# Loading queries and keys in token order for an attention stage ahead of two feed-forward layers

## The chip, the cores and the metric

The kernel runs on one core of a Trainium2 chip. The metric is the time of one execution on the device in microseconds (us); less is better. Below, TensorE is the engine for matrix products and transposes, VectorE, ScalarE and GpSimd do elementwise work, and SP is the queue from which most transfers are started. In rows of the profile they are called PE (weight loads: PEld), DVE, ACT, POOL and SP.

## The reference

For 4 batches, 8 heads, 576 tokens and head dimension 64, two attentions are added; then two feed-forward layers follow on 2304 tokens of width 512 with 2048 hidden features.

```python
q_d = q.reshape(B, H, Sd, factor, D).mean(axis=3)      # factor = 4; k_d, v_d in the same way
out_up = np.repeat(sm_attn(q_d, k_d, v_d), factor, axis=2)
mask = np.abs(pos[:, None] - pos[None, :]) < factor
scores = np.where(mask, scale * np.matmul(q, k.transpose(0, 1, 3, 2)), -1000000000.0)
out_local = np.matmul(softmax(scores), v)
x = out_up + out_local                                  # then, for each layer:
h = x @ w_in                                            # g = h * sigmoid(h) in layer 1, elu(h) in layer 2
return g @ w_out
```

The weights come as float64.

## The kernel before

The attention is done for 16 pairs of heads: pair i is two heads of one batch, whose 64 dimensions each lie on partitions 0 to 63 and 64 to 127. `attention(i)` is a generator; each `yield` ends one step, and `step()` takes one step of each live pair in turn. The first four pairs (batch 0) run side by side at the start, each begun three steps behind the one before, with matrix products of zeros between them (`warm`). Then the feed-forward layers begin, and the steps of pairs 4 to 15 are put between their matrix products by `tick`: one at a time in the first two blocks of tokens and three at a time after that. A pair has 19 steps.

The feed-forward products are done by `g1` (line 452) and `g2` (lines 503 and 505) on weights that are kept as two parts. The weights are turned from float64 to float32 by `decode_w` (lines 152 to 159 on VectorE, 143 on ScalarE) and split by `split_w` (169 and 171); the first 16 tiles of them are prepared during the first attention pairs and the first block.

The order of the instructions on every engine is the order in which the program gives them; nothing is reordered, so an instruction that waits holds back all behind it on its engine. Transfers on SP and on ScalarE's queue are started in that order too.

What the change touches in `attention`:

- `load_rows` loads queries (which = 0), keys (1) and values (2) of a pair: eight neighbouring tokens on each of 72 partitions. For the first four pairs a partition gets runs of 2 KB, and `set_beside` (line 220, VectorE) copies them so that the two heads' dimensions lie side by side. From pair 4 on the load itself sets them side by side, in runs of 256 bytes.
- 16 transposes of 72 tokens (line 281, tile `pst`, four to a PSUM bank), four copies out of PSUM with a stride (line 282, ScalarE), and two sums over four tokens (line 288, VectorE) give `qT`, `kT` and the pooled `qD`, `kD`.
- GpSimd adds the values (lines 296 and 297: `vt`, `vd`). After these the loads of the next pair are started.
- `psl` (line 308) holds the banded scores: 20 products whose operands lie alternately on the two halves of the partitions and whose results go alternately to two halves of PSUM's partitions.
- The pooled scores `psd` (line 334): for each head two products over 64 partitions and then a maximum on VectorE (341) that is scaled by a separate instruction (344) before ScalarE's exponential (347).
- The tiles `qT`, `kT`, `vt`, `E`, `ED`, `aT` and `aD` share seven buffers (`ring`); a tile waits until a buffer is free.
- `psu` (line 391) holds the weighted pooled values: four products of 72 partitions whose results go in turn to the two halves of PSUM's partitions.

Of the kernel before, what the change touches and what calls it, by code (L numbers as in the profile page):

```python
# [21 lines left out]
def attention_moe_moe2_kernel(ctx, tc, q, k, v, wi1, wo1, wi2, wo2, out):  # L22
# [10 lines left out]
    NBS = (2 * P, 3 * P)  # tokens of a block in each layer  # L33
# [5 lines left out]
    PSCALE = SCALE / (FAC * FAC)  # L39
    EPS = 1e-9  # L40
    MASKED = -1e9
    WIN = 64
    PACES = (1.0, 0.9, 0.7)  # steps of attention per tick in the first block, the second and the others
    DECODE_PACE = 1.5  # small steps of the first weights per tick
    N_EARLY = 9  # tiles of weights that may be prepared before the first product
    WARM, FILL = 9, (8, 4, 4, 4)
    GROUP = 3  # steps of attention at a time after the first two blocks
    LAG = 3  # tiles of hidden features between the two products
    # 2^16 times the float32 whose bits are the high word of the float64 that is float32's largest.
# [4 lines left out]
    # Windows of the banded attention: key start, query start, first useful query of each.  # L54
# [27 lines left out]
    def constants():  # L82
# [24 lines left out]
    # Tiles of weights in the order of their use; each is loaded, decoded and split in turn.  # L107
# [72 lines left out]
    # The first batch's four pairs go side by side and borrow memory that is not in use yet: tokens  # L180
    # of the later batches in x32, the parts of x, and the partial results.
    borrowed = {}

    def borrow(i, name):
        at, n = {"qT": (S, S), "kT": (2 * S, S), "qD": (3 * S, SD), "kD": (3 * S + SD, SD), "vd": (3 * S + 2 * SD, 2 * SD)}[name]
        return x32[:, pairs[i][1], at:at + n][:, :2 * 2 * D if name == "vd" else n]

    def load_rows(i, which, engine=None):
        b, h0 = pairs[i][0], 2 * pairs[i][1]
        src = (q, k, v)[which]  # L190
        if i in (1, 2) and which < 2:
            t = xs.tile([P, KC * NBM], F32R, tag=("xh", "xl")[which], name=f"rows{which}").bitcast(F32)
            borrowed[2 * i - 2 + which] = t
            t = t[:, :4 * FAC * D].rearrange("p (r e) -> p r e", e=2 * D)
        elif i == 3 and which == 0:
            borrowed["y"] = yp.tile([P, 4 * NBM], F32, tag="y", name="rows0")
            t = borrowed["y"][:, :4 * FAC * D].rearrange("p (r e) -> p r e", e=2 * D)
        else:
            t = nat.tile([P, 2 * FAC, 2 * D], F32, tag="nat", name=f"rows{which}", bufs=3)
        # Eight neighbouring tokens on a partition; the two heads' dimensions of q and k side by side.  # L200
        if which == 2 or i < NPAIR:
            t = t.rearrange("p r e -> p (r e)").rearrange("p (h e) -> p h e", h=2)
            (engine or nc.sync).dma_start(t[:HS], src[b, h0:h0 + 2].rearrange("h (p r) d -> p h (r d)", r=2 * FAC))
        else:
            (engine or nc.sync).dma_start(
                t[:HS].rearrange("p r (h d) -> p r h d", h=2),
                src[b, h0:h0 + 2].rearrange("h (p r) d -> p r h d", r=2 * FAC),
            )
        loaded[i, which] = t

    # The first batch's rows come whole, a head after the other, for its loads are waited for.
    beside = {}

    def set_beside(i, which):
        src = loaded[i, which].rearrange("p h (a r d) -> p a r h d", a=2, r=FAC)
        for a in range(2):
            tag = ("wh0", "wl0", "wh1", "wl1")[2 * which + a]
            t = wpool.tile([P, DM], F32R, tag=tag, name="beside").bitcast(F32).rearrange("p (r e) -> p r e", r=FAC)
            beside[i, which, a] = t
            nc.vector.tensor_copy(t[:HS].rearrange("p r (h d) -> p r h d", h=2), src[:HS, a])  # L220
# [39 lines left out]
    def ring(name, n):  # L260
        return att.tile([P, NW * WIN], F32, tag="ring", name=name, bufs=7)[:, :n]

    def attention(i):
        b, pr = pairs[i]
        # Transposes: dimensions of both heads on the partitions, tokens along the row.
        tT = []
        tD = []
        if i < NPAIR:
            set_beside(i, 0)
            set_beside(i, 1)  # L270
        for which, nm in enumerate("qk"):
            src = loaded.pop((i, which))
            t = borrow(i, f"{nm}T") if i < NPAIR else ring(f"{nm}T", S)
            for a in range(2):
                if i < NPAIR:
                    rows = beside[i, which, a]
                else:
                    rows = src[:, a * FAC:(a + 1) * FAC, :]
                ps = bank("pst")
                for r in range(FAC):  # L280
                    nc.tensor.transpose(ps[:, r * HS:(r + 1) * HS], rows[:HS, r, :], ident[:HS, :HS])  # L281
                nc.scalar.copy(
                    t.rearrange("p (m a r) -> p a r m", a=2, r=FAC)[:, a],
                    ps[:, :HALF].rearrange("p (r m) -> p r m", r=FAC),
                )
                yield
            d = borrow(i, f"{nm}D") if i < NPAIR else att.tile([P, SD], F32, tag=f"{nm}D", name=f"{nm}D")
            nc.vector.reduce_sum(d, t.rearrange("p (m r) -> p m r", r=FAC), axis=AX.X)
            tT.append(t)
            tD.append(d)  # L290
        # Values pooled over FAC neighbours (their sum).
        vt = ring("vt", 2 * 2 * 2 * D).rearrange("p (n r d) -> p n r d", n=4, r=2)
        vd = borrow(i, "vd") if i < NPAIR else att.tile([P, 4 * D], F32, tag="vd", name="vd", bufs=3)
        vd = vd.rearrange("p (n d) -> p n d", n=4)
        vn = loaded.pop((i, 2)).rearrange("p h (a r d) -> p (h a) r d", a=2, r=FAC)
        nc.gpsimd.tensor_tensor(vt[:HS], vn[:HS, :, 0:2, :], vn[:HS, :, 2:4, :], ALU.add)
# [5 lines left out]
        # Banded scores, two windows of queries stacked on the partitions.  # L302
# [11 lines left out]
        for j in range(2):  # L314
            nc.vector.scalar_tensor_tensor(
                E[:, :, j, :], psl[j][:, :NW // 2 * WIN].rearrange("p (s w) -> p s w", w=WIN), SCALE, mask,
# [9 lines left out]
        # Pooled scores.  # L326
# [4 lines left out]
        for j in range(2):  # L331
            ps = bank("psd")
            for a in range(2):
                nc.tensor.matmul(  # L334
                    ps[:HS, a * SD:(a + 1) * SD],
# [3 lines left out]
                )  # L339
            nm = att.tile([P, 2], F32, tag="nm", name="nm", bufs=4)  # L340
# [3 lines left out]
            nc.vector.tensor_scalar_mul(nm[:HS], nm[:HS], PSCALE)  # L344
            yield
            for a in range(2):
                nc.scalar.activation(
                    ED[:HS, j, a, :], ps[:HS, a * SD:(a + 1) * SD], AF.Exp, bias=nm[:HS, a:a + 1], scale=PSCALE,
# [9 lines left out]
        # The pooled values are sums of FAC: their factor goes into the weights.  # L358
# [8 lines left out]
        # Weights transposed: keys on the partitions.  # L367
# [18 lines left out]
        # Weighted values; dimensions of both heads on the partitions.  # L386
# [56 lines left out]
    def g1(u, tick):  # L443
# [17 lines left out]
        if layer == 0:  # L461
            # 2 silu(h) = (tanh(h / 2) + 1) h
# [3 lines left out]
        else:  # L466
            # elu(h) = max(exp(min(h, 0)) - 1, h)
# [11 lines left out]
    def g2(u, tick):  # L479
# [53 lines left out]
    with tc.manual_schedule():  # L533
# [10 lines left out]
        # Products of zeros keep TensorE at its full clock where it has nothing else to do yet.  # L544
# [8 lines left out]
        # Work that is spread between the matrix products, a small step at a time.  # L553
# [26 lines left out]
        # The first tiles of weights: decoded and split at once, two of them in turn.  # L580
# [34 lines left out]
        def step():  # L615
            # Some pairs in turn, each some stages behind the one before.
# [48 lines left out]
        def advance():  # L665
            # The rest of a tile's elementwise work, a step at a time.
# [93 lines left out]
```

## Time and profile before

| what | value |
|---|---|
| time, median of 3 runs | 1003.09 us (1002.03 to 1005.25) |
| span of the profiled execution, first to last instruction | 1000.2 us |
| TensorE busy | 970.6 us, 97% |
| VectorE busy | 583.9 us, 58% |
| ScalarE busy | 429.2 us, 43% |
| GpSimd busy | 368.8 us, 37% |
| mean granted TensorE clock | 0.970 |

The profile prints no time of the profiled execution but its span; the median of the runs is 2.9 us above that. Busy time is counted for each engine from its own instructions. Shares over the whole span mix stages with different limits, so a stage is read by its own stretch of time. A matmul's length in the timeline overlaps with the next one, so the price of a matmul is read from the distance between starts.

### The profile page before, as it was taken

To read this page: it belongs to the slowest core of one execution; us is meant where nothing else is said; L and a number is where in the kernel's file an instruction comes from. 1 tells how busy PE (TensorE), PEld (TensorE's weight loads), DVE (VectorE), ACT (ScalarE), POOL (GpSimd) and SP (SyncE) were. 2 spreads that over 40 slices of the span, in tenths; PEclk is the share of its full clock that TensorE was granted. 3 is DMA by queue.
4 is the path that set the end of the run, shared out by engine and by line. 5 is a ranking of instruction groups with operands and counts; after the bars stand their busy time and mean duration, and the time that the engine had idled before them with its cause. 6 is when DMAs were issued, how large, how long until landed. Compare 5 with 4: busy or idle time off the path is not lost.

```text
span 1000.2 us, 18822 instructions
## 1 busy us (share of the span) xinstructions
PE 970.6 (97%) x7517; PEld 893.8 (89%) x7517; DVE 583.9 (58%) x1076; ACT 429.2 (43%) x1032; POOL 368.8 (37%) x375
## 2 busy tenths in 40 slices
PE   7887799999999999999999999999999999999998
PEld 4567688999999999999999999999999999999997
DVE  7999864555548966876322267677643544434432
ACT  4555546456445556444333354333333533223321
POOL 3756654543522235222222362222223622222221
PEclk9677799999999999999999999999999999999999
DMA  8555644333205541343100001232000011101111
GB/s 210 129 131 134 155 96 107 84 75 88 62 8 154 182 130 56 117 125 117 53 23 22 22 22 43 78 112 64 32 32 32 1 64 64 44 20 64 64 38 57
DMA packets 81687, 77.76 MB, mean 78 GB/s; under 512 B 51520, under 2 KB 67904, under 8 KB 81600
## 3 DMA queue, kind: packets, MB, share of 16 engines
q1 hardware_dynamic: 81288, 75.97, 26.6%
q8 instruction: 59, 0.97, 0.4%
q10 hardware_dynamic: 312, 0.59, 0.2%
q14 instruction: 28, 0.23, 0.1%
HBM read 62.39 MB, written 14.16 MB: 77 GB/s over the span
## 4 chain that ended last, share of the span: by engine, by line
PE 89%; DVE 8%; DMA 1%; issue 1%; ACT 1%; POOL 0%; ACTq 0%; DVEq 0%; POOLq 0%
PE ph L452 40%; PE y L503 21%; PE y L505 20%; PE pso L403 2%; PE psd L334 1%; PE pst L281 1%; DVE wf L157 1%; DVE wf L152 1%; DVE wf L153 1%; DMA rows<-in_k_dram 1%; PE psl L308 1%; DVE wf L159 1%; PE psu L391 1%; DVE nm L344 1%; PE psE L374 1%
## 5 line engine op out<-in xcount | busy, mean ns | idle before, releaser
L475 POOL TENSOR_TENSOR gl<-t,gh 128x256 fp32r<-128x256 f32 (+1 forms) x240 | 215.9, 900 | 527.2 <-ACT gh L473 514.0
L452 PE MATMUL ph<-xh,wh 128*128 128x256 f32 (+1 forms) x960 | 279.4, 309 | 1.6 <-DVE t L465 1.6
L452 PE MATMUL ph<-xl,wh 128*128 128x256 f32 (+1 forms) x960 | 278.8, 308 | 0.0
L452 PEld LDWEIGHTS ph<-xh,wh 128*128 128x128 f32 x960 | 183.9, 192 | 7.9 <-DVE t L465 1.8
L452 PEld LDWEIGHTS ph<-xl,wh 128*128 128x128 f32 x960 | 184.0, 192 | 4.6 <-issue 0.4
L452 PE MATMUL ph<-xh,wl 128*128 128x256 f32 (+1 forms) x960 | 179.9, 307 | 0.3 <-POOL wl L171 0.3
L503 PE MATMUL y<-gh,wh 128*128 128x256 f32 x576 | 169.3, 294 | 0.0
L473 ACT CAST gh<-t 128x256 fp32r<-128x256 f32 (+1 forms) x240 | 107.9, 449 | 132.8 <-DVE t L465 83.8
L503 PE MATMUL y<-gl,wh 128*128 128x256 f32 x576 | 163.9, 285 | 0.0
L503 PE MATMUL y<-gh,wl 128*128 128x256 f32 x576 | 163.8, 284 | 0.0
L452 PEld LDWEIGHTS ph<-xh,wl 128*128 128x128 f32 x960 | 149.6, 192 | 1.3 <-POOL wl L171 0.6
L465 DVE SCALAR_TENSOR_TENSOR t<-t,ph 128x256 f32<-128x256 f32 x144 | 60.1, 418 | 141.8 <-ACT t L463 141.6
L469 ACT ACTIVATE t<-t 128x384 f32<-128x384 f32 x96 | 50.5, 526 | 211.1 <-DVE t L468 211.0
L468 DVE TENSOR_SCALAR t<-ph 128x384 f32<-128x384 f32 x96 | 53.4, 556 | 126.1 <-PE ph L452 126.0
L503 PEld LDWEIGHTS y<-gh,wh 128*128 128x128 f32 x576 | 111.4, 193 | 3.7 <-issue 3.1
L505 PE MATMUL y<-wl,gh 128*128 128x512 f32 x288 | 113.9, 396 | 0.0
L505 PE MATMUL y<-wh,gl 128*128 128x512 f32 x288 | 113.7, 395 | 0.0
L463 ACT ACTIVATE t<-ph 128x256 f32<-128x256 f32 x144 | 55.5, 385 | 133.1 <-PE ph L452 130.2
L505 PE MATMUL y<-wh,gh 128*128 128x512 f32 x288 | 111.9, 389 | 0.0
L503 PEld LDWEIGHTS y<-gl,wh 128*128 128x128 f32 x576 | 111.5, 194 | 0.0
L503 PEld LDWEIGHTS y<-gh,wl 128*128 128x128 f32 x576 | 111.4, 193 | 0.0
L471 DVE SCALAR_TENSOR_TENSOR t<-t,ph 128x384 f32<-128x384 f32 x96 | 53.2, 554 | 56.8 <-ACT t L469 56.8
(89 smaller groups left out, 1306.8 us busy)
## 6 DMA issues: line engine op xcount, KB each, us to landing
ws<-in_moe_w_in_dram SPq DMA_DIRECT2D x32, 512.0 KB
ws<-in_moe_w_out_dram SPq DMA_DIRECT2D x32, 512.0 KB
rows<-in_q_dram SPq DMA_DIRECT2D x16, 288.0 KB
rows<-in_v_dram SPq DMA_DIRECT2D x16, 288.0 KB
yp<-yo SPq DMA_DIRECT2D x9, 512.0 KB
part<-yp SPq DMA_DIRECT2D x9, 512.0 KB
yp<-yo SPq DMA_DIRECT2D x6, 768.0 KB
part<-yp SPq DMA_DIRECT2D x6, 768.0 KB
```

The costliest lines, as they stand in the source:

```text
L152: nc.vector.tensor_scalar(tf, tf, 2.0, W_MAX, op0=ALU.max, op1=ALU.min)
L403: nc.tensor.matmul(ps[j * D:(j + 1) * D, o:o + n], loaded[i, 3][j * WIN:(j + 1) * WIN, w, :], aT[j * WIN:(j + 1) * WIN, w // 2, c0:c0 + n] ...
L452: nc.tensor.matmul(ph[:, :nb], a[:, c, :], b[:, c, :], start=k == 0, stop=k == 3 * KC - 1)
L463: nc.scalar.activation(t, h, AF.Tanh, scale=0.5)
L465: nc.vector.scalar_tensor_tensor(t, t, 1.0, h, op0=ALU.add, op1=ALU.mult)
L468: nc.vector.tensor_scalar_min(t, h, 0.0)
L469: nc.scalar.activation(t, t, AF.Exp)
L471: nc.vector.scalar_tensor_tensor(t, t, -1.0, h, op0=ALU.add, op1=ALU.max)
L473: nc.scalar.copy(gh, t)
L475: nc.gpsimd.tensor_tensor(gl, t, gh.bitcast(F32), ALU.subtract)
L503: nc.tensor.matmul(y[d // 2][:, h:h + nb], wm[:, sl], gm, start=first and d % 2 == 0, stop=last, skip_group_check=True)
L505: nc.tensor.matmul(y[d], gm[:, sl], wm, start=first, stop=last)
```

## The change

- Queries and keys are loaded in token order: tokens 0 to 95 on 96 partitions, the next 96 beside them and so on, six groups, with the two heads side by side. Each head is a load of its own, in runs of 256 bytes; that holds for the first four pairs too. `set_beside` and its copies go.
- Twelve transposes of 96 tokens (five of the queries, five of the keys, then one of each) replace sixteen of 72, in three steps in place of four. Their results are in token order, so the copies out of PSUM write without a stride: 480, 480, 96 and 96 columns. The copies of the queries multiply by the pooled scale.
- One sum over four tokens makes both pooled tiles. The banded scores are scaled by 16 times less, to fit the scaled queries; the pooled scores need no scale, and line 344 goes.
- The values of a pair are loaded a head at a time and added by two GpSimd instructions of half the size in place of one.
- The pooled scores of both heads are computed in one step, the heads in turn, each into its own PSUM bank; the two maxima stay in their steps.
- `nat` has 2 buffers and `natv` 1 in place of 3 of `nat`; `ring` has 5 in place of 7 since queries and keys have a tile `qk` of their own; `vd` has 2 in place of 3.

```diff
     def load_rows(i, which, engine=None):
...
+        if which == 2:
+
+            if i < NPAIR:
+                heads = [wpool.tile([P, DM], F32R, tag=tag, name="rows2").bitcast(F32) for tag in ("wh0", "wl0")]
+            else:
+                t = nat.tile([P, 4 * FAC * D], F32, tag="natv", name="rows2", bufs=1)
+                heads = [t[:, :DM], t[:, DM:]]
+            for j, t in enumerate(heads):
+                (engine or nc.sync).dma_start(t[:HS], src[b, h0 + j].rearrange("(p r) d -> p (r d)", r=2 * FAC))
+            loaded[i, which] = heads
+            return
...
-            t = nat.tile([P, 2 * FAC, 2 * D], F32, tag="nat", name=f"rows{which}", bufs=3)
...
+            t = nat.tile([P, NTB * 2 * D], F32, tag="nat", name=f"rows{which}", bufs=2)
+        t = t[:, :NTB * 2 * D].rearrange("p (c e) -> p c e", c=NTB)
+        for j in range(2):
+            (engine or nc.sync).dma_start(t[:TB, :, j * D:(j + 1) * D], src[b, h0 + j].rearrange("(c p) d -> p c d", p=TB))
...
-        return att.tile([P, NW * WIN], F32, tag="ring", name=name, bufs=7)[:, :n]
+        return att.tile([P, NW * WIN], F32, tag="ring", name=name, bufs=5)[:, :n]
...
-            set_beside(i, 0)
-            set_beside(i, 1)
...
+        for parts in ([(0, c) for c in range(NTB - 1)], [(1, c) for c in range(NTB - 1)], [(0, NTB - 1), (1, NTB - 1)]):
+            ps = bank("pst")
+            for n, (which, c) in enumerate(parts):
+                nc.tensor.transpose(ps[:, n * TB:(n + 1) * TB], rows[which][:TB, c, :], ident[:TB, :TB])
...
+                    if which == 0:
+                        nc.scalar.activation(dst, ps[:, o:o + n], AF.Copy, scale=PSCALE)
+                    else:
+                        nc.scalar.copy(dst, ps[:, o:o + n])
+                    o += n
+            yield
+        nc.vector.reduce_sum(qkD, qk.rearrange("p (m r) -> p m r", r=FAC), axis=AX.X)
...
-        nc.gpsimd.tensor_tensor(vt[:HS], vn[:HS, :, 0:2, :], vn[:HS, :, 2:4, :], ALU.add)
+        for j, vn in enumerate(loaded.pop((i, 2))):
+            vn = vn.rearrange("p (a r d) -> p a r d", a=2, r=FAC)
+            nc.gpsimd.tensor_tensor(vt[:HS, 2 * j:2 * j + 2], vn[:HS, :, 0:2, :], vn[:HS, :, 2:4, :], ALU.add)
...
-        for j in range(2):
-            ps = bank("psd")
-            for a in range(2):
+        psd = [bank("psd"), bank("psd")]
+        for a in range(2):
+            for j in range(2):
                 nc.tensor.matmul(
-                    ps[:HS, a * SD:(a + 1) * SD],
+                    psd[j][:HS, a * SD:(a + 1) * SD],
                     qD[j * D:(j + 1) * D, a * HS:(a + 1) * HS],
                     kD[j * D:(j + 1) * D, :],
                     start=True, stop=True,
                 )
...
-            nc.vector.tensor_scalar_mul(nm[:HS], nm[:HS], PSCALE)
```

## Rows read from the trace of the kernel before

**Rows 1.** Windows of four stretches: start:end, length, busy per engine, granted clock, DMA share, GB/s.
```profile
10.00:62.00 52.00, 44.02 (x474) 29.33 (x471) 49.68 (x92) 28.63 (x78) 31.17 (x24) 0.74 0.60 152
62.00:120.00 58.00, 43.30 (x424) 36.93 (x421) 54.05 (x91) 29.87 (x78) 35.34 (x28) 0.78 0.59 146
120.00:292.00 172.00, 171.79 (x2052) 157.57 (x2052) 95.69 (x215) 93.95 (x270) 83.15 (x85) 0.99 0.34 81
292.00:600.00 308.00, 308.00 (x2551) 308.00 (x2552) 180.73 (x334) 137.70 (x334) 105.45 (x122) 1.00 0.27 83
```

**Rows 2.** Chain that ended last, start and length in us: first and last psd of 18.
```profile
134.13 0.64 PE psd L334 x4
...
275.46 0.64 PE psd L334 x4
```

**Rows 3.** Timeline of TensorE matmuls: start, length in us, line, operation, tiles, shapes, count.
```profile
150.24 0.28 PE L503 MATMUL y<-gh,wl 128*128 128x256 f32 x1
150.44 0.71 PE L334 MATMUL psd<-kD,qD 64*72 64x144 f32 x4
151.08 0.39 PE L503 MATMUL y<-gh,wh 128*128 128x256 f32 x1
151.31 0.28 PE L503 MATMUL y<-gl,wh 128*128 128x256 f32 x1
151.42 0.28 PE L503 MATMUL y<-gh,wl 128*128 128x256 f32 x1
151.54 0.42 PE L281 MATMUL pst<-ident,rows 72*128 72x72 f32 x4
...
151.96 0.28 PE L503 MATMUL y<-gl,wh 128*128 128x256 f32 x1
...
158.45 0.71 PE L391 MATMUL psu<-aD,vd 72*64 72x144 f32 x8
159.09 0.39 PE L452 MATMUL ph<-xl,wh 128*128 128x256 f32 x1
...
160.00 0.81 PE L308 MATMUL psl<-kT,qT 64*64 64x64 f32 x40
```

**Rows 4.** Windows of line 344 alone on VectorE.
```profile
24.60:62.00 37.40, 4.08 (x5) 0.66 0.48 115
62.00:120.00 58.00, 5.11 (x6) 0.78 0.59 146
```

**Rows 5.** Windows of line 220 alone on VectorE.
```profile
5.00:24.60 19.60, 7.44 (x16) 0.95 0.91 233
```

**Rows 6.** Timeline of GpSimd and VectorE round one small scaling.
```profile
41.71 1.26 POOL L323 TENSOR_TENSOR E<-E,mx 128x640 f32<-128x640 f32 x1 [4.08 <-DVE mx L322]
...
42.03 0.96 DVE L344 TENSOR_SCALAR nm<-nm 72x2 f32<-72x2 f32 x1
```

**Rows 7.** Groups by line and shape: busy us, mean ns, idle before.
```profile
L282 ACT COPY qT<-pst 128x288 f32<-128x288 f32 x24 | 17.0, 710 | 10.2 <-PE pst L281 10.2
...
L288 DVE TENSOR_REDUCE qD<-qT 128x144 f32<-128x576 f32 x12 | 9.0, 747 | 5.1 <-ACT qT L282 5.1
```

**Rows 8.** Timeline: first GpSimd addition of values, first row sum of pair 0.
```profile
16.91 1.27 POOL L296 TENSOR_TENSOR vt<-rows 72x512 f32<-72x512 f32 x1 [13.23 <-DMA rows<-in_v_dram]
...
24.61 0.80 DVE L354 TENSOR_REDUCE rl<-E 128x10 f32<-128x640 f32 x1
```

**Rows 9.** Windows of the first loads, and of loads in 256-byte runs.
```profile
2.00:13.00 11.00, 8.23 (x85) 4.42 (x83) 7.14 (x23) 4.67 (x7) 1.48 (x7) 1.00 0.85 211
24.00:25.00 1.00, 1.00 (x28) 0.88 (x21) 1.00 (x4) 0.00 (x0) 0.00 (x0) 0.50 1.01 130
```

**Rows 10.** Line 230 on the load queue: issue time min/median/max in ns.
```profile
L230 SPq DMA_DIRECT2D vw<-in_v_dram x28: 608/626/1738, 21.8 to 273.6; - x28
```

**Rows 11.** Timeline of ScalarE: copies for pair 1 and pair 0.
```profile
36.56 0.48 ACT L375 COPY aT<-psE 128x384 f32<-128x384 f32 x1 [0.60 <-PE psE L374]
...
40.11 0.26 ACT L394 COPY up<-psu 128x144 f32<-128x144 f32 x1
```

More of the change, by code (lines that the diff above doesn't have):

```diff
@@ L39, in attention_moe_moe2_kernel @@
     PSCALE = SCALE / (FAC * FAC)
+    BSCALE = SCALE / PSCALE
+    TB = 96
+    NTB = S // TB
     EPS = 1e-9
@@ L184, in borrow @@
     def borrow(i, name):
-        at, n = {"qT": (S, S), "kT": (2 * S, S), "qD": (3 * S, SD), "kD": (3 * S + SD, SD), "vd": (3 * S + 2 * SD, 2 * SD)}[name]
+        at, n = {"qk": (S, 2 * S), "qkD": (3 * S, 2 * SD), "vd": (3 * S + 2 * SD, 2 * SD)}[name]
         return x32[:, pairs[i][1], at:at + n][:, :2 * 2 * D if name == "vd" else n]
@@ L190, in load_rows @@
         src = (q, k, v)[which]
-        if i in (1, 2) and which < 2:
+        if which == 2:
[8 more added lines that the diff above has]
+            return
@@ L192, in load_rows @@
+        if i in (1, 2):
             t = xs.tile([P, KC * NBM], F32R, tag=("xh", "xl")[which], name=f"rows{which}").bitcast(F32)
             borrowed[2 * i - 2 + which] = t
-            t = t[:, :4 * FAC * D].rearrange("p (r e) -> p r e", e=2 * D)
         elif i == 3 and which == 0:
             borrowed["y"] = yp.tile([P, 4 * NBM], F32, tag="y", name="rows0")
-            t = borrowed["y"][:, :4 * FAC * D].rearrange("p (r e) -> p r e", e=2 * D)
+            t = borrowed["y"]
         else:
-            t = nat.tile([P, 2 * FAC, 2 * D], F32, tag="nat", name=f"rows{which}", bufs=3)
@@ L201, in load_rows @@
[L201 to L208, printed above, removed]
-        loaded[i, which] = t
-    beside = {}
@@ L214, in set_beside @@
-    def set_beside(i, which):
-        src = loaded[i, which].rearrange("p h (a r d) -> p a r h d", a=2, r=FAC)
-        for a in range(2):
[L217 to L220, printed above, removed]
+            t = nat.tile([P, NTB * 2 * D], F32, tag="nat", name=f"rows{which}", bufs=2)
@@ L260, in ring @@
     def ring(name, n):
-        return att.tile([P, NW * WIN], F32, tag="ring", name=name, bufs=7)[:, :n]
+        return att.tile([P, NW * WIN], F32, tag="ring", name=name, bufs=5)[:, :n]
     def attention(i):
         b, pr = pairs[i]
-        tT = []
-        tD = []
         if i < NPAIR:
-            set_beside(i, 0)
-            set_beside(i, 1)
[L271 to L290, printed above, removed]
@@ new lines, in attention @@
+            qk = borrow(i, "qk")
+            qkD = borrow(i, "qkD")
+        else:
+            qk = att.tile([P, 2 * S], F32, tag="qk", name="qk")
+            qkD = att.tile([P, 2 * SD], F32, tag="qkD", name="qkD")
+        rows = [loaded.pop((i, which)) for which in range(2)]
+        tT = [qk[:, :S], qk[:, S:]]
+        tD = [qkD[:, :SD], qkD[:, SD:]]
+        for parts in ([(0, c) for c in range(NTB - 1)], [(1, c) for c in range(NTB - 1)], [(0, NTB - 1), (1, NTB - 1)]):
+            ps = bank("pst")
+            for n, (which, c) in enumerate(parts):
+                nc.tensor.transpose(ps[:, n * TB:(n + 1) * TB], rows[which][:TB, c, :], ident[:TB, :TB])
+            o = 0
+            for which in range(2):
+                n = TB * sum(w == which for w, _ in parts)
+                if n:
+                    c0 = TB * min(c for w, c in parts if w == which)
+                    dst = tT[which][:, c0:c0 + n]
+                    if which == 0:
+                        nc.scalar.activation(dst, ps[:, o:o + n], AF.Copy, scale=PSCALE)
+                    else:
+                        nc.scalar.copy(dst, ps[:, o:o + n])
+                    o += n
+            yield
@@ L292, in attention @@
+        nc.vector.reduce_sum(qkD, qk.rearrange("p (m r) -> p m r", r=FAC), axis=AX.X)
         vt = ring("vt", 2 * 2 * 2 * D).rearrange("p (n r d) -> p n r d", n=4, r=2)
-        vd = borrow(i, "vd") if i < NPAIR else att.tile([P, 4 * D], F32, tag="vd", name="vd", bufs=3)
+        vd = borrow(i, "vd") if i < NPAIR else att.tile([P, 4 * D], F32, tag="vd", name="vd", bufs=2)
         vd = vd.rearrange("p (n d) -> p n d", n=4)
-        vn = loaded.pop((i, 2)).rearrange("p h (a r d) -> p (h a) r d", a=2, r=FAC)
@@ L315, in attention @@
             nc.vector.scalar_tensor_tensor(
-                E[:, :, j, :], psl[j][:, :NW // 2 * WIN].rearrange("p (s w) -> p s w", w=WIN), SCALE, mask,
+                E[:, :, j, :], psl[j][:, :NW // 2 * WIN].rearrange("p (s w) -> p s w", w=WIN), BSCALE, mask,
                 op0=ALU.mult, op1=ALU.add,
@@ L330, in attention @@
         rl = att.tile([P, NW, 1], F32, tag="rl", name="rl", bufs=4)
-        for j in range(2):
-            ps = bank("psd")
-            for a in range(2):
+        psd = [bank("psd"), bank("psd")]
+        for a in range(2):
+            for j in range(2):
                 nc.tensor.matmul(
-                    ps[:HS, a * SD:(a + 1) * SD],
+                    psd[j][:HS, a * SD:(a + 1) * SD],
                     qD[j * D:(j + 1) * D, a * HS:(a + 1) * HS],
@@ L339, in attention @@
                 )
+        for j in range(2):
+            ps = psd[j]
             nm = att.tile([P, 2], F32, tag="nm", name="nm", bufs=4)
@@ L347, in attention @@
                 nc.scalar.activation(
-                    ED[:HS, j, a, :], ps[:HS, a * SD:(a + 1) * SD], AF.Exp, bias=nm[:HS, a:a + 1], scale=PSCALE,
+                    ED[:HS, j, a, :], ps[:HS, a * SD:(a + 1) * SD], AF.Exp, bias=nm[:HS, a:a + 1],
                     accum_out=sm[:HS, 2 * j + a:2 * j + a + 1],
```

## The prediction

> **What bounds the kernel now.** I read the windows first, cut where the limits change. From 10 to 120 us VectorE is busy for 103.7 of 110 us, at a granted TensorE clock of 0.74 and 0.78, a mean over stretches at its two levels, 2.4 and 1.2 GHz; TensorE is idle for 15% and 25% in these stretches. From 120 us to the end of attention TensorE is busy for 171.8 of 172 us at clock 0.99, and after that without a gap [rows 1]. So there are two prices. Before 120 us a microsecond of VectorE's time is worth something, and after 120 us only TensorE's is. The chain of waits says the same: before 120 us it runs mostly over VectorE's lines, after that over TensorE's products, with the pooled scores `psd` of nine pairs (7 to 15) on it, 18 pieces of 0.64 us [rows 2]. Busy matmul time is modelled, so I price matmuls by distances between starts in the timeline.
>
> **Pooled scores.** A block of `psd` (one head) lasts 0.64 us to the next start, the product ahead of it takes 0.20 us and the one behind it 0.23, where such a product else takes 0.11 to 0.12. One block thus costs 0.64 + 0.08 + 0.11 = 0.83 us, two of them 1.66 a pair [rows 3]. Four matmul records of 144 columns in 0.64 us are 160 ns each, so one after another. `psu` has eight records of the same 144 columns in 0.64 us (158.45 to 159.09), 80 ns each: its products alternate between two halves of the output partitions and overlap in twos. `psl`, which alternates between halves of the input too, has 40 records of 64 columns in some 0.74 us, 18.5 ns each: 0.29 ns a column, where `psd` has 1.11 and `psu` 0.56 [rows 3]. That is four at once, so halves of the input overlap as well when their results go to different banks. The new order gives `psd` just that: heads in turn, a bank each. I take one block of eight records at `psu`'s price, 0.64 + 0.19 = 0.83 us, and save 0.83 a pair. If nothing overlaps, only one pair of gaps is saved, 0.19. Nine pairs: **7.5 us**, bounds 1.7 and 7.5. This comes straight off the end, since no other engine is over 56% busy there [rows 1].
>
> **Transposes.** Four of 72 columns and one product last from 151.54 to 151.96, so the four cost 0.30 us and a pair's sixteen 1.20 [rows 3]. Twelve of 96 stream the same 1152 columns. If the price goes by columns, only one step's gap of about 0.08 goes; if by instruction, a quarter goes, 0.30. A loss I exclude: neither columns nor instructions rise. I take 0.1, for 72 columns in some 55 to 75 ns look like streaming. Nine pairs: **0.9 us**, bounds 0.7 and 2.7.
>
> **VectorE before 120 us.** Line 344 is a scaling of 72x2 numbers, but takes 4.08 us in five runs from 24.6 to 62 us and 5.11 us in six from 62 to 120 [rows 4]. The long ones end with a GpSimd instruction: the subtraction on `E` runs from 41.71 to 42.97, the scaling from 42.03 to 42.99 [rows 6]. What follows a scaling is mostly a sum or a two-input operation, which in this trace run beside GpSimd; so I count the wait as gone, not as moved to the next. The copies of `set_beside` take 7.44 us in 5 to 24.6 us [rows 5], but there the data and the values are late too (below), so I count none of that beyond what covers the later loads. The two sums of 0.75 us [rows 7] become one of twice the length: at most 0.1 a pair, put at nothing. So 9.2 us of VectorE's time goes after 24.6 us. Not all of it shortens the chain: products, exponentials and weight splits stand between. Before 62 us I take nearly all, 3.5 of 4.08; from 62 on, where TensorE too is at work for 43.3 of 58 us, 3 of 5.11. Bounds: nothing, and all of it with the copies beside, 16.6.
>
> **Loads at the start.** The first eight loads of queries and keys are 2.36 MB in runs of 2 KB; from 2 to 13 us 211 GB/s move, which is these loads [rows 9]. Now they come in runs of 256 bytes. The nearest row is the second from 24 us, when chiefly the value windows, in runs of 256 bytes, were in flight: 130 GB/s at full DMA share [rows 9]. Bounds: 211 GB/s (no loss) and 130 (18.1 us in place of 11, 7 later). I take 160, for part of that second may be a tail: 14.7 us, 3.7 later. Pair 0 needs only the first quarter and loses its copies, so it starts about as before. But its values come behind all eight loads: GpSimd waits 13.23 us for them and adds at 16.91, and only then subtracts on `E` for the exponential whose row sum VectorE makes at 24.61 [rows 8]. At 20.6 the values' additions and the subtraction take some 3.5 us, the exponential 0.75: the row sum comes at about 25, some 0.3 later. Behind the waiting addition on GpSimd stand the additions and subtractions of pairs 1 and 2, behind the exponential on ScalarE the copies of pairs 2 and 3; VectorE would idle there, which is where its saved copies go. Issuing costs 0.63 us a head in 256-byte runs [rows 10], twelve on SP and four on ScalarE's queue: 7.6 us on SP, ahead of the data's rate. The last keys wait for pair 0's transposes to free their buffer, at some 8 us, while earlier loads still move, so they lose nothing.
>
> The Trainium skill's page "DMA: Bandwidth & Descriptors" (section Specifications) asks for at least 512 bytes in a transfer for the full rate, which speaks against this change. Its section "Why a DMA increments its semaphore by 16 and not by 1" speaks for it: the engines used divide the number of partitions, so 12 for 72 and 16 for 96. By that second rule alone an estimate is a third more rate, 281 GB/s, and 2.6 us gained; the page has no price for the first. The trace agrees that 256-byte runs move fewer bytes at full share; no run here shows 96 partitions yet.
>
> **Fewer buffers, ScalarE, GpSimd.** With five `ring` buffers pair 1's first copy of `aT` (36.56 us) finds none free until pair 0's `psu` is done, which is copied at 40.11 [rows 11]. ScalarE can stall up to 3 us there, with weight copies behind it; I charge 1, bounds 0 and 3. Later a buffer is free at least two steps ahead. ScalarE's copies get shorter (four of 0.71 us go [rows 7]) but it is not the limit. GpSimd gets one more fixed start a pair. Both I put at nothing, covered by TensorE from 120 us on; without that cover GpSimd's would be some 0.2 us a pair. Next-pair loads on SP issue some 1 us longer a pair, but are asked for seven or more steps ahead.
>
> **Sum.** 7.5 + 0.9 + 3.5 + 3 - 0.3 - 1 = 13.6 us. The profiled span of 1000.2 becomes 986.6; with the 2.9 us by which the median lies above it, 989.5, put at **989 us**.
>
> **Rivals.**
> - *Pooled scores don't overlap.* For it: their result is 72 partitions wide, more than half of TensorE's columns, and `psl` and `psu` have 64. Against it: `psl`'s 18.5 ns needs overlap of input halves. Only 1.7 of 7.5 us stay: 995.
> - *The start gives nothing back.* VectorE's waits for GpSimd move to the next scaling of weights, or the clock stays at 1.2 GHz longer. For it: weight scalings at lines 152 and 153 are on the chain there too. The 5.2 us of the start (3.5 + 3 - 0.3 - 1) go: 994.7.
> - *The start gives all.* The copies count too and the loads lose nothing: 16.6 in place of 5.2 us: 978.
> - *Slower: the short runs hold up the start.* The rule on 512 bytes as a mechanism here: all first pairs wait for loads, VectorE idles, and nothing catches up. At 130 GB/s it costs 3.3 us more than charged: 993. It cancels the whole gain when the loads end some 17 us later than now (13.6 plus the 3.7 charged), at 30 us rather than 13, some 83 GB/s; from 20 us later, 75 GB/s, it is slower than 1006. No row at full share is so low, but many short loads were never in flight alone. I give that 1010.
>
> **Chances.** Forecast (985 to 992) 0.44; no overlap 0.13; start gives nothing 0.19; start gives all 0.12; start held up 0.12, of which 0.07 slower and 0.04 about even. A difference of 0.3%, 3 us, is about what a measurement can tell from none. Some weight of the second and third cases falls within it when both hold, 0.05 together. So faster 0.84, same 0.09, slower 0.07. The range reaches up past both weak cases and down to the case that the start gives all: 979 to 999.
>
> **What would show it.** Right: two `psd` blocks become one of about 0.64 us; the stretch from the first full-clock product to the end of attention is 8 us shorter; line 344 is gone and no other VectorE line has grown by as much; the first addition of values comes at about 20 us; TensorE is without gaps from about 115 us. Wrong: a `psd` block of 1.2 us or more, GpSimd adding values after 25 us, a longer stretch at 1.2 GHz before 120 us, or waits of ScalarE on `aT`.

## The result and the profile after

| | before | after |
|---|---|---|
| time, median | 1002.64 us (1002.03 to 1005.25, 4 runs) | 991.29 us (990.9 to 991.39, 4 runs) |
| span of the profiled execution | 1000.2 us | 989.4 us |
| mean granted TensorE clock | 0.970 | 0.972 |

The ratio is 0.9871 (95% interval 0.985 to 0.9892): the change gains 11.35 us by the medians, 10.8 by the spans. The forecast was 989, its own range 985 to 992. The time lies in that range, 2.3 us above the figure. Four of the terms did not come as forecast (below) and their errors cancelled in part, so that the sum held is partly luck.

Windows of the kernel after (start:end, length, busy time of PE, PEld, DVE, ACT and POOL, granted clock, DMA share, GB/s), the first for [rows 9], the others for [rows 1]:

```profile
2.00:13.00 11.00, 10.38 (x132) 5.87 (x131) 6.85 (x17) 4.93 (x13) 1.50 (x7) 1.00 1.28 221
10.00:62.00 52.00, 40.39 (x422) 27.09 (x422) 42.13 (x73) 26.36 (x82) 29.47 (x28) 0.74 0.59 150
62.00:120.00 58.00, 44.21 (x481) 38.90 (x477) 54.49 (x82) 30.60 (x91) 40.65 (x33) 0.79 0.65 162
120.00:292.00 172.00, 170.06 (x2032) 158.54 (x2032) 93.38 (x201) 85.63 (x268) 85.41 (x95) 0.99 0.33 84
```

In the window of the first loads 221 GB/s move where 211 moved before, so that runs of 256 bytes are no slower in sum. The DMA share rose from 0.85 to 1.28, which is 44% more for each byte moved. From 10 to 62 us VectorE is now busy for 42.13 of 52 us (49.68 before), so it no longer fills this stretch; something else holds it there. From 62 to 120 us it is as full as before.

TensorE's timeline after (start, length in us; distances between starts count):

```profile
148.19 0.28 PE L504 MATMUL y<-gh,wl 128*128 128x256 f32 x1
148.32 0.58 PE L276 MATMUL pst<-ident,rows 96*128 96x96 f32 x5
148.68 0.36 PE L504 MATMUL y<-gh,wh 128*128 128x256 f32 x1
148.88 0.28 PE L504 MATMUL y<-gl,wh 128*128 128x256 f32 x1
...
150.14 0.33 PE L276 MATMUL pst<-ident,rows 96*128 96x96 f32 x2
150.25 0.36 PE L453 MATMUL ph<-xl,wh 128*128 128x256 f32 x1
150.45 0.28 PE L453 MATMUL ph<-xh,wh 128*128 128x256 f32 x1
...
157.93 0.71 PE L334 MATMUL psd<-qkD 64*72 64x144 f32 x8
158.57 0.62 PE L453 MATMUL ph<-xh,wl 128*128 128x256 f32 x3
```

A `psd` block now has eight records in 0.64 us, where two blocks of four took 0.64 each [rows 3]. Five transposes and one product take 0.56 us (148.32 to 148.88); less 0.12 for the product that is 0.44, and in the same way two transposes cost 0.19. A pair's twelve cost 2 × 0.44 + 0.19 = 1.07 us, against 1.20 before.

The start, in timelines of GpSimd, VectorE, ScalarE and TensorE (the arrow names what ended the idle time before the row), for [rows 8]:

```profile
14.95 1.41 POOL L296 TENSOR_TENSOR vt<-rows 72x256 f32<-72x256 f32 x2 [11.25 <-DMA rows<-in_v_dram]
...
19.18 0.82 DVE L355 TENSOR_REDUCE rl<-E 128x10 f32<-128x640 f32 x1 [2.71 <-ACT E L353]
...
32.19 0.72 POOL L297 TENSOR_TENSOR x<-vt 72x256 f32<-72x256 f32 x1
...
32.94 0.40 ACT L385 COPY aD<-psD 72x288 f32<-72x288 f32 x1 [6.18 <-POOL x L297]
...
33.39 1.23 PE L334 MATMUL psd<-x 64*72 64x144 f32 x6 [2.74 <-ACT aD L385]
...
34.65 0.43 DVE L156 TENSOR_SCALAR wf<-wf 128x512 f32<-128x512 f32 x1 [3.78 <-ACT wf L147]
```

The first addition of values begins at 14.95 us, 1.96 earlier than before, and the row sum of pair 0 comes at 19.18, 5.4 earlier. Then most of it is lost in one place: ScalarE waits 6.18 us, until GpSimd has added the values of pair 3 and so frees a `ring` buffer for pair 0's `aD`. Behind that copy stand the exponentials and the weight copies of ScalarE, so VectorE idles 3.78 us and TensorE 2.74.

Where the gain arises is read from VectorE's copies of finished output tiles, the first ones of the first, fifth, sixth and last block of tokens. Before, line 515:

```profile
147.81 0.68 DVE L515 TENSOR_SCALAR yo<-y 128x512 f32<-128x512 f32 x1
...
299.62 0.68 DVE L515 TENSOR_SCALAR yo<-y 128x512 f32<-128x512 f32 x1
323.26 0.68 DVE L515 TENSOR_SCALAR yo<-y 128x512 f32<-128x512 f32 x1
...
801.73 1.28 DVE L515 TENSOR_SCALAR yo<-y 128x512 f32<-128x512 f32 x2
```

After, line 516:

```profile
144.85 0.68 DVE L516 TENSOR_SCALAR yo<-y 128x512 f32<-128x512 f32 x1
...
289.02 0.68 DVE L516 TENSOR_SCALAR yo<-y 128x512 f32<-128x512 f32 x1
312.43 0.68 DVE L516 TENSOR_SCALAR yo<-y 128x512 f32<-128x512 f32 x1
...
790.92 1.28 DVE L516 TENSOR_SCALAR yo<-y 128x512 f32<-128x512 f32 x2
```

The gain is 2.96 us at the end of the first block, 10.60 at the fifth, 10.83 at the sixth and 10.81 at the last. So the start gave 3 us, the stretch in which TensorE is the bound 7.9, and what follows nothing.

### The profile page after: what moved, and what is told of

It reads as the page before. It is cut to its first block, busy times and chain, and to the rows that moved or that the text cites. A ratio compares the mean times of both kernels' runs of the same rounds, so it can differ in the third digit from the quotient of the medians.

```text
span 989.4 us, 18693 instructions
## 1 busy us (share of the span) xinstructions
PE 956.6 (97%) x7453; PEld 884.8 (89%) x7453; DVE 563.5 (57%) x1012; ACT 412.4 (42%) x1032; POOL 372.7 (38%) x391
## 4 chain that ended last, share of the span: by engine, by line
PE 88%; DVE 8%; issue 1%; ACT 1%; DMA 1%; POOL 1%; SPq 0%; DVEq 0%; POOLq 0%; ACTq 0%
PE ph L453 41%; PE y L504 21%; PE y L506 20%; PE pso L404 2%; PE pst L276 1%; DVE wf L163 1%; DVE wf L161 1%; PE psu L392 1%; PE psl L308 1%; DVE wf L156 1%; PE psE L375 1%; PE psD L384 1%; DVE wf L157 1%; DVE rl L356 1%; DVE rl L355 1%
```

## Experiments

Eleven kernels were run. Times are medians; a median of the kernel before, run along with them, lay between 1001.95 and 1004.63 us, so that a difference of 1 to 2 us between kernels of different groups says little by itself. For small differences spans and block ends stand beside it. A span is that of one profiled run, and in every run the time is 1.8 us above the span. That one run was the shortest of its kernel's runs for the kernel before (of the four above) and for both kernels with the scaling back, and the longest for "the same, and the factor" and for "values later and own room"; so a difference of spans carries an error of 1 to 2 us too.

| kernel | us | ratio to before (95%) | span |
|---|---|---|---|
| before with heads in turn | 995.1 | 0.9922 (0.9903 to 0.9941) | 993.1 |
| the same, and the factor | 991.95 | 0.9894 (0.9879 to 0.9909) | 991.3 |
| after | 991.29 | 0.9871 (0.985 to 0.9892) | 989.4 |
| after, one head, then the other | 991.13 | 0.9871 (0.9853 to 0.9889) | 989.2 |
| after, one half of the input | 994.07 | 0.9917 (0.99 to 0.9935) | 992.2 |
| after, scaling back | 994.11 | 0.9903 (0.9886 to 0.992) | 990.5 |
| after, own room for value sums | 987.81 | 0.9838 (0.982 to 0.9856) | 986.0 |
| own room and scaling back | 992.11 | 0.9897 (0.9879 to 0.9916) | 988.1 |
| after, loads cut 72 + 24 | 993.21 | 0.991 (0.9891 to 0.9929) | 991.0 |
| after, loads cut 48 + 48 | 994.89 | 0.9924 (0.9908 to 0.9941) | 993.3 |
| after, values added later | 989.02 | 0.9863 (0.9847 to 0.9878) | 987.6 |
| values later and own room | 985.62 | 0.9832 (0.9815 to 0.9849) | 985.2 |

**Pooled scores alone.** The kernel before with only its `psd` part changed:

```diff
-        for j in range(2):
-            ps = bank("psd")
-            for a in range(2):
+        psd = [bank("psd"), bank("psd")]
+        for a in range(2):
+            for j in range(2):
                 nc.tensor.matmul(
-                    ps[:HS, a * SD:(a + 1) * SD],
+                    psd[j][:HS, a * SD:(a + 1) * SD],
...
+        for j in range(2):
+            ps = psd[j]
```

> The kernel before with one part of the change alone: the pooled scores of both heads in one step, heads in turn, a bank each. If the overlap is the cause of the gain after 130 us, the time falls by 9 x 0.83 = 7.5 us there and perhaps 0.5 before it: some 995 us. If it needs the other parts, it stays within 1 us of 1002.6 us.

The time is 995.1 us; the span falls from 1000.2 to 993.1, by 7.1 us. This is the term of 7.5.

**Does it need the turn?** The changed kernel with the two products of one head first:

```diff
-        for a in range(2):
-            for j in range(2):
+        for j in range(2):
+            for a in range(2):
```

> The changed kernel with one thing undone: the pooled scores of a pair still come in one step and in two banks, but first both products of one head, then both of the other. If overlap of the two halves of the partitions makes the gain after 130 us, a block of eight records lasts about 1.28 us instead of 0.64 and the time rises by 9 x 0.64 = 5.8 us, to some 997 us. If the gain there comes from having one block instead of two (fewer gaps), or from the transposes, the time stays at 991 to 992 us.

TensorE's timeline of this kernel:

```profile
157.68 0.72 PE L334 MATMUL psd<-qkD 64*72 64x144 f32 x8
158.33 0.62 PE L453 MATMUL ph<-xh,wl 128*128 128x256 f32 x3
```

The time is 991.13 us, the same as 991.29, and a block is still eight records with 0.65 us to the next start. The order inside the block is not what matters. The expectation had supposed that this order undoes the overlap; as it doesn't, this run can't tell overlap from fewer gaps, and the next one has to.

**Does it need both halves?**

```diff
-                    qD[j * D:(j + 1) * D, a * HS:(a + 1) * HS],
-                    kD[j * D:(j + 1) * D, :],
+                    qD[0:D, a * HS:(a + 1) * HS],
+                    kD[0:D, :],
```

> The changed kernel, but all four pooled products of a pair read head 0's half of the partitions (the pooled scores of head 1 are left out), in the same order and into the same two banks. Theory of the prediction (the two halves of the input work side by side): without a second half a block of eight records takes two times 0.64 us = 1.28 us in place of 0.64 to 0.71, so nine pairs cost 0.6 us each more in the stretch in which TensorE is the bound: 5 to 6 us, about 997. Rival (one block costs about 0.64 us whatever is in it, as a fixed price of a block that is paid once in place of twice): the block stays at 0.65 to 0.7 us and the time at 991.

TensorE's timeline of this kernel:

```profile
157.21 1.20 PE L334 MATMUL psd<-qkD 64*72 64x144 f32 x8
158.34 0.62 PE L453 MATMUL ph<-xh,wl 128*128 128x256 f32 x3
```

The block takes 1.13 us to the next start in place of 0.64, so the halves of the input do work side by side. The rival, a fixed price of a block, falls. The time rose by 2.8 us and not by 5 to 6: I had counted nine pairs, but in the changed kernel only seven `psd` blocks come after the first block of tokens. From the first block's end to the sixth's is 171.05 us against 167.58, and 7 × 0.49 = 3.4 is nearly that difference of 3.5.

**The small scaling.** The changed kernel, with line 344 put back:

```diff
+            nc.vector.tensor_scalar_mul(nm[:HS], nm[:HS], 1.0)
             yield
```

> The changed kernel with the small scaling on VectorE put back behind each maximum (times one). If the waits for GpSimd that line 344 bore had only moved to other scalings (line 356 of the changed kernel took 467 ns instead of 209), it costs little: 1 us or less, 992 us. If they were really gone, as the prediction counted, it costs 5 to 6.5 us: 996.5 to 998 us.

It gave 994.11 us, 2.8 more by the median and 1.1 by the span, between the two theories. Was the gain small because the wait for the ring buffer lay behind it? So the same was done where that wait is gone, with the room of the next experiment:

> The changed kernel with the sums of the first four pairs' values in room of their own, and besides with the scaling of line 344 put back as a product with 1.0. It asks whether line 344 was worth little (2.8 us by the median, 1.05 by the profile) only because the wait for the ring buffer lay behind it. Theory (VectorE's waits for GpSimd went from line 344 to the next scaling, line 356 above all, so they are mostly moved): 1 to 3 us more than with own room alone, 989 to 991, and line 356 falls from a mean of 423 ns towards 390 or less. Rival (the missing buffer hid the gain, as the prediction's 6.5 us would have it): 5 us or more above own room alone, 993 or more.

It gave 992.11 us, 4.3 over own room alone by the median (outside of the theory's 1 to 3 and short of the rival's 5) and 2.1 by the span (988.1 against 986.0); its runs scatter from 989.88 to 993.02. The missing buffer may have hidden a part, 4.3 against 2.8 us, but not as much as the rival needs. What tells more is where VectorE's waits went. Groups of VectorE's instructions from 24 to 120 us (count | busy us, mean ns | idle before), first own room alone, then with the scaling back:

```profile
L157 DVE TENSOR_SCALAR wf<-wf 128x512 int32<-128x512 int32 x16 | 15.7, 983 | 0.5
L161 DVE SCALAR_TENSOR_TENSOR wf<-ws,wf 128x512 int32<-128x512 int32 x16 | 15.0, 942 | 0.0
L356 DVE TENSOR_SCALAR rl<-rl 128x10 f32<-128x10 f32 x6 | 2.8, 462 | 0.2
```

```profile
L157 DVE TENSOR_SCALAR wf<-wf 128x512 int32<-128x512 int32 x16 | 12.6, 790 | 0.6
L161 DVE SCALAR_TENSOR_TENSOR wf<-ws,wf 128x512 int32<-128x512 int32 x16 | 12.0, 757 | 0.0
L346 DVE TENSOR_SCALAR nm<-nm 72x2 f32<-72x2 f32 x10 | 8.5, 854 | 0.3
L357 DVE TENSOR_SCALAR rl<-rl 128x10 f32<-128x10 f32 x6 | 2.3, 383 | 0.2
```

With the scaling, it takes 8.5 us, and three other groups take 15.7 - 12.6 + 15.0 - 12.0 + 2.8 - 2.3 = 6.6 us less. So 6.6 of 8.5 us only move when it goes; 1.9 stay. Of the 6.6, 3.1 go to line 157, a scaling of weights with one input (line 153 of the kernel before), and 3.0 to line 161 with two. One such move in the timelines of VectorE and GpSimd, again first without and then with the scaling:

```profile
39.53 1.32 POOL L363 TENSOR_TENSOR rows<-rows,sm 72x576 f32<-72x576 f32 x1
40.81 1.26 POOL L175 TENSOR_TENSOR wl<-wf,wh 128x512 fp32r<-128x512 f32 x1
...
39.77 0.44 DVE L343 TENSOR_REDUCE nm<-psd 72x2 f32<-72x288 f32 x1
40.14 2.49 DVE L161 SCALAR_TENSOR_TENSOR wf<-ws,wf 128x512 int32<-128x512 int32 x1
```

```profile
42.42 1.26 POOL L175 TENSOR_TENSOR wl<-wf,wh 128x512 fp32r<-128x512 f32 x1
...
41.37 0.44 DVE L343 TENSOR_REDUCE nm<-psd 72x2 f32<-72x288 f32 x1
41.85 1.85 DVE L346 TENSOR_SCALAR nm<-nm 72x2 f32<-72x2 f32 x1
43.61 0.68 DVE L161 SCALAR_TENSOR_TENSOR wf<-ws,wf 128x512 int32<-128x512 int32 x1
```

1.85 + 0.68 us became 2.49 in one instruction, a two-input operation on weights. In each case GpSimd is at work until the wait ends: until 42.07 us, 0.56 before line 161 is done, and until 43.68, when the scaling is done. The Trainium skill has the rule on the page "SBUF — State Buffer" (section "Who interferes with whom"): a VectorE instruction with both inputs in SBUF contends with a GpSimd instruction that reads SBUF. The trace agrees, 2.49 us against 0.68 for the same instruction; the prediction had taken the opposite. It had read rows of the kernel before like these:

```profile
42.91 1.28 DVE L157 SCALAR_TENSOR_TENSOR wf<-ws,wf 128x512 int32<-128x512 int32 x2
...
42.93 2.38 POOL L171 TENSOR_TENSOR wl<-wf,wh 128x512 fp32r<-128x512 f32 x1
```

VectorE's two-input operations keep their length here, 0.64 us each, but they began first, and it is GpSimd's subtraction that takes 2.38 us, where another of its kind takes 1.27 at 58.06.

**The factor alone, on the kernel before.** Heads in turn as above, and

```diff
-                nc.scalar.copy(
+                nc.scalar.activation(
...
+                    AF.Copy, scale=(PSCALE, 1.0)[which],
...
-            nc.vector.tensor_scalar_mul(nm[:HS], nm[:HS], PSCALE)
```

with the banded scores and the exponential scaled to match.

> The kernel before with the pooled scores of both heads in turn and the pooled factor carried by the queries (so without its line 344); loads, transposes, copies and the seven ring buffers stay as they were. Theory (the factor alone gives 1 to 3 us): 992 to 994, against 995.1 with the heads in turn alone; what is left to 991.3 is then what loads, transposes, copies and buffers give in sum, some 1 to 3 us. Rival (as predicted, line 344 gives some 6.5 us where no buffer is missing, and the new loading and the five buffers lose what it gives): 988 to 989.

It gave 991.95 us, 3.2 below the heads in turn alone, 1.8 by the spans (993.1 and 991.3). The rival's 988 to 989 falls: no buffer is missing here, and the gain is still 3.2 us. The same groups from 24 to 120 us, first with the scaling, then without:

```profile
L159 DVE SCALAR_TENSOR_TENSOR wf<-ws,wf 128x512 int32<-128x512 int32 x15 | 12.9, 869 | 0.0
L346 DVE TENSOR_SCALAR nm<-nm 72x2 f32<-72x2 f32 x11 | 9.6, 870 | 0.4
```

```profile
L159 DVE SCALAR_TENSOR_TENSOR wf<-ws,wf 128x512 int32<-128x512 int32 x15 | 18.8, 1267 | 0.0
```

Line 159 alone takes 5.9 of the 9.6 us back.

**The missing buffer.** The value sums of the first four pairs get room of their own, in tiles for weights that are not in use yet:

```diff
-        vt = ring("vt", 2 * 2 * 2 * D).rearrange("p (n r d) -> p n r d", n=4, r=2)
+        vt = (wpool.tile([P, DM], F32R, tag="wl1", name="vt").bitcast(F32) if i < NPAIR else ring("vt", 2 * 2 * 2 * D)).rearrange("p (n r d) -> p n r d", n=4, r=2)
```

> The changed kernel with the sums of values (vt) of the first four pairs in memory of the weights that is not in use yet, so that five ring buffers are shared by fewer tiles. If the 6.2 us in which ScalarE waits at 26.8 us for GpSimd's addition of pair 3 (to get a ring buffer for aD) set back the start, the wait goes and the time falls by 2 to 4 us, to 987 to 989 us. If that wait is hidden behind VectorE or the loads, the time stays at 991 us.

It gave 987.81 us, 3.5 less than the change, by the spans 3.4. The place is right too, for the copy of `aD` no longer waits for GpSimd. ScalarE's timeline:

```profile
28.38 0.39 ACT L385 COPY aD<-psD 72x288 f32<-72x288 f32 x1 [0.66 <-PE psD L384]
```

**What set the loads' rate.** The DMA share of 1.28 against 0.85 suggested that 96 partitions use more DMA engines than 72. Test and control cut each load of queries and keys of the first four pairs in two:

```diff
-            (engine or nc.sync).dma_start(t[:TB, :, j * D:(j + 1) * D], src[b, h0 + j].rearrange("(c p) d -> p c d", p=TB))
+            for lo, hi in ((0, 72), (72, 96)) if i < NPAIR else ((0, 96),):
+                (engine or nc.sync).dma_start(t[lo:hi, :, j * D:(j + 1) * D], src[b, h0 + j].rearrange("(c p) d -> p c d", p=TB)[lo:hi])
```

> The changed kernel, but each load of queries and keys of the first four pairs is cut in two, 72 and 24 partitions, still in runs of 256 bytes. Theory (the loads kept their rate because 96 partitions are spread over 16 DMA engines and 72 over 12, which the DMA share of 1.28 against 0.85 speaks for): the stretch from 2 to 13 us shows 165 to 190 GB/s in place of 221, the first addition of values begins at 17 to 19 us in place of 14.95, and the time is 1 to 3 us longer, 992 to 994. Rival (runs of 256 bytes at 96 partitions cost nothing special, the rate is set by something else, memory or the issue of loads): 210 to 225 GB/s, the same start, 991.

This looked like the theory: 181 GB/s, share 0.80, first addition at 17.13 us, 993.21. But it also issues twice as many loads, so the control cuts at 48:

> The changed kernel, but each load of queries and keys of the first four pairs is cut in two halves of 48 partitions. It is the control for the cut into 72 and 24: as many loads to issue, as many bytes, runs of 256 bytes, but by the rule that the engines divide the partitions each half goes over 16 engines and not over 12. Theory (the number of engines sets the rate): the DMA share from 2 to 13 us comes back to 1.2 to 1.3 and the rate to 210 to 225 GB/s, the first addition of values to 15 to 16 us, the time to 991 to 992. Rival (the cut kernel was slower because it issued twice as many loads): 175 to 190 GB/s at a share near 0.8, first addition at 17 us, 993, as with 72 and 24.

First the cut at 72, then the control, in windows:

```profile
2.00:13.00 11.00, 9.27 (x89) 4.98 (x88) 5.47 (x16) 3.83 (x8) 1.50 (x7) 1.00 0.80 181
```

```profile
2.00:13.00 11.00, 9.20 (x89) 4.98 (x88) 5.57 (x16) 3.93 (x9) 1.48 (x7) 1.00 0.92 177
```

The control does not bear my theory out: with 48 and 48 the rate is no better, the first addition comes at 19.22 us, and the time is 994.89. What the two cuts share is the number of loads. In the control the DMA share falls to 0.27, at 57 GB/s, from 13 to 15 us, while SP is still issuing the last queries and keys, so there the issue, or a wait of the queue, holds the transfers up. The queue's timeline, after and with the cut at 72:

```profile
9.41 1.22 SPq L217 DMA_DIRECT2D rows<-in_k_dram  x2
10.68 1.96 SPq L203 DMA_DIRECT2D rows<-in_v_dram  x4
```

```profile
12.32 1.73 SPq L218 DMA_DIRECT2D rows<-in_k_dram  x4
14.09 1.62 SPq L203 DMA_DIRECT2D rows<-in_v_dram  x4
```

SP issues loads from 0.74 us on with hardly a gap, and the values' loads stand behind all of them: from 10.68 us after, from 14.09 with 24 issues in place of 12 (from 15.77 in the control). Before, SP had issued the first values much earlier:

```profile
6.56 0.97 SPq L203 DMA_DIRECT2D rows<-in_v_dram  x2
```

Yet they were added at 16.91 us, later than after the change. Up to that point 3.3 MB had moved before; after the change it was 2.9 MB up to 14.95 us, both at a mean of 196 GB/s. So the values did not come earlier by a higher rate; it is likely, but not shown, that fewer bytes of weights and later values moved beside them, as SP issued those later too. How much of 221 GB/s comes from more engines stays open; the rule on engines that the prediction cites from the Trainium skill's page "DMA: Bandwidth & Descriptors" (section "Why a DMA increments its semaphore by 16 and not by 1") is neither shown nor refuted by a run here.

The two kernels give a price besides: with the loads later, so that the first addition of values comes 2.18 and 4.27 us later, the time rises by 1.9 and 3.6 us, 0.88 and 0.84 us for each. This is an estimate, for the cuts delay more than the values: ScalarE issues its share of the loads until 6.5 and 6.4 us in place of 2.9.

**Not waiting for the values.** For the first four pairs GpSimd adds the values behind its other work:

```diff
+        def add_values():
+            vt = ring("vt", 2 * 2 * 2 * D).rearrange("p (n r d) -> p n r d", n=4, r=2)
...
+        if i >= NPAIR:
+            add_values()
...
             ED3[:HS], ED3[:HS], sm.rearrange("p (n o) -> p n o", o=1)[:HS].to_broadcast([HS, 4, SD]), ALU.mult
         )
+        if i < NPAIR:
+            add_values()
```

> The changed kernel, but for the first four pairs GpSimd adds the values behind its work on the scores, so that the subtraction on the band's scores does not stand behind the values' load. Theory (the start is now held by GpSimd: pair 0's subtraction waits for the values, and ScalarE later waits 6.18 us for the addition of pair 3, which holds a ring buffer): subtraction of pair 0 before 12 us in place of 17, its row sum at 14 to 16 us in place of 19.2, no wait of ScalarE on the addition, and 986 to 989. Rival (VectorE's work in the start is what counts, and it is only shifted): the row sum comes earlier, the wait on the ring is gone, but the time is 990 to 992.

> As the kernel with the values added later, and besides the sums of the first four pairs' values lie in room of their own and not in a ring buffer. Theory (both the wait for the values and the missing buffer cost time, 3.4 us the second alone): 984 to 987, lower than the kernel with own room alone (987.8). Rival (the missing buffer was all that there was to get): 987 to 988.5, the same as with own room alone.

The subtraction for pair 0 begins at 11.27 us (17.12 in the change), its row sum at 16.88, later than expected. The wait on the ring stayed, 5.58 us, against what I expected: the addition now comes at another step, but still holds the buffer. 989.02 is at the upper edge of the theory. With room as well it is 985.62 us, the fastest kernel here, 17 us below before. Its step beyond own room alone is 2.2 us by the medians but 0.8 by the spans; that this part pays without the ring's is likely, its size isn't settled.

## Why the prediction was right, and where its steps failed

By the spans the gain splits into 7.1 us for the heads in turn (1000.2 to 993.1), 1.8 for the factor (to 991.3) and 1.9 for loads, transposes, copies and buffers together (to 989.4); by the medians, into 7.5, 3.2 and 0.7. The first output copies of the first and the sixth block tell where: with the heads in turn (146.64 and 316.16 us) 1.2 us come up to the first block's end and 5.9 between the two, with the factor besides (144.74 and 314.32) another 1.9 and nothing. All the rest gives nothing up to the first block's end and 2.0 after it, where one pair fewer is left to do: seven `psd` blocks in place of eight.

| step | predicted | measured |
|---|---|---|
| pooled scores | 7.5 | 7.1 |
| transposes | 0.9 | 0.13 a pair, 1.2 for nine |
| line 344 | 3.5 + 3 | about 3 (2.8, 3.2, 4.3 by medians; 1.1, 1.8, 2.1 by spans) |
| loads | -0.3 | not slower; values 1.96 us earlier, some 1.7 by the price above (an estimate) |
| ring of five buffers | -1 (0 to -3) | -3.4, as what own room gave back |
| copies of `set_beside` and the rest | 0 | not measured; left over are 2.4 by spans (1.9 + 3.4 - 1.2 - 1.7) and 1.3 by medians (0.7 + 3.5 - 1.2 - 1.7) |

- *Pooled scores: right, in size and cause.* The inference from `psl`, that halves of the input overlap, holds, and 5.9 us on the eight pairs behind the first block are 0.74 a pair. Its lower bound was wrong: it supposed that one block in place of two saves only 0.19 us. The run with one half has 1.13 + 0.19 = 1.32 us a pair against 1.66, so a single block saves 0.34, and the halves the other 0.49.
- *Line 344: the step that failed* is "I count the wait as gone, not as moved to the next". It was taken from the belief that two-input operations run beside GpSimd. In these runs they wait for it or make it wait, and the decoding of weights that follows consists of them and of scalings. So 6.5 us were counted where about 3 came, and 6.6 of the 8.5 us of the scaling moved. The rival that VectorE's waits move to the next scaling of weights named line 153, which took 3.1 of the 6.6, and was mostly right in mechanism, though the start as a whole gave 3 us.
- *Loads: the sign was wrong.* The nearest row, one microsecond of value windows at 130 GB/s, was no measure for these loads. The issue was too small in the prediction: 7.6 us on SP, where it took 9.9 (0.74 to 10.63). Even so the values came 1.96 us earlier in place of 3.7 later, at the same mean rate up to then; why is not shown. The Trainium skill's page "DMA: Bandwidth & Descriptors" (section Specifications) asks for 512 bytes for the full rate. In this case 256-byte runs moved 221 GB/s against 211 in 2 KB runs, so that no loss shows in the rate; whether the 44% more of DMA share for each byte is the price of short runs, and more engines at work cover it, no run here separates. The prediction says that this page has no price for short runs; it does give an overhead for 256 bytes, in its section "Why small descriptors are slow (HBM only)".
- *Ring: the mechanism was right, tile and size were wrong.* It named `aT`, which waits only 0.78 us. It was `aD` of pair 0, which waits until the values of pair 3 are added, and it cost 3.4 us where the bound was 3. The changed kernel with seven buffers was not run.
- *The signs it gave.* One `psd` block of 0.64 us: seen. A stretch 8 us shorter: 7.9, though one pair fewer lies after the first block. No other VectorE line longer: wrong. The first addition of values at about 20 us: it came at 14.95. TensorE without gaps from 115 us: nearly, 170.06 of 172 us from 120 on.

## What to carry to other kernels

When a VectorE instruction mostly waits for GpSimd, removing it is worth only what the next instructions don't wait in its place: list which of them share that limit before counting the time as gained. When buffers are cut, go through all tiles that take one in the order of the program, and look for one whose last reader stands far back in an engine's queue. And before a second theory rests on an experiment, look for what else the edit changed: the control with 48 and 48 partitions took back a conclusion that its sibling had seemed to prove.

## What was unexpected of the hardware

- Two `psd` products of one half and two of the other overlap whatever their order in the program: 0.65 us for the block, against 1.13 with one half only.
- While queries and keys come in 256-byte runs on 96 partitions, 221 GB/s move at a DMA share of 1.28; in 2 KB runs on 72 it was 211 at 0.85.
- Cutting loads in two so that more are issued costs time even when bytes and runs are the same: 221 GB/s became 181 and 177.
